# A state-space and feed-forward block on one core: an earlier load, late modulation in steps, and an engine for each PSUM copy

## The chip, the core and the metric

The kernel runs on one core of a Trainium2 chip. The core has a matrix engine (TensorE, PE in the profile; PEld is its weight load), a vector engine (VectorE, DVE), a scalar engine (ScalarE, ACT), GpSimd (POOL) and SyncE (SP), which here only issues transfers. Each engine works through its own instructions in order and waits for others by semaphores. Matmul results land in PSUM, which has banks of 128 x 512 fp32 values; VectorE and ScalarE carry them from there to SBUF. The metric is the device time of one execution in microseconds, as the median of several runs.

## The reference

```python
mod = (silu(c) @ w_mod).reshape(1, 6, 1, -1)
sa, ca, ga, sb, cb, gb = (mod[:, i] for i in range(6))
h = layernorm(x) * (1 + ca) + sa                  # x: 1 x 2048 x 512
x = x + ga * S4(h)
h = layernorm(x) * (1 + cb) + sb
x = x + gb * ((relu(h @ w1 + b1) ** 2) @ w2 + b2) # w1: 512 x 1792

def S4(u):                                        # 512 channels, 128 states each
    dt = exp(log_dt)
    P = exp(dt * A * l)                           # complex A, l = 0 .. 2047
    K = real(sum over n of C * P * (dt * B))      # one kernel of 2048 per channel
    return causal_convolution(u, K) + u * Dskip
```

All values are fp32.

## The kernel before

**Head.** `log_dt` (`ldt`), the vector c (`cin`), the S4 parameters (`prm`, one part of 64 channels and one of 448) and sixteen rows of x are loaded. VectorE forms dt = exp(log_dt) in 14 small operations (L455 to L465); a matmul group (L468) and a ScalarE copy (L471) spread it. `parameters()` (L476 to L542) then makes, from A, B, C and dt, a decay rate, a phase and an amplitude per state, in fp32 products on GpSimd, reciprocals and comparisons on VectorE, and Abs, Sign, Arctan and Sin on ScalarE; it is run for the first 64 channels and for the other 448. Beside it VectorE takes the layernorm statistics of the sixteen rows (L556, L557), and TensorE forms the first three modulation vectors from `w_mod` (L579), which become a gain and a shift per channel (L611 to L616). Sixteen row steps follow (`row_pieces`, L626 to L634): VectorE applies mean, gain and shift, TensorE transposes, ScalarE copies the bank into `xj`. Every block of 64 channels needs all sixteen rows.

**Convolution.** It is done by matmuls against fixed tables of cosines, in 8 blocks of 64 channels. For each block `u_pieces` (capitals A to H) transforms the input in four `stage1` steps (8 matmuls with `d1`, L668, and a bank copy, L670) and four `stage2` steps (16 matmuls with `t2`, L678, and a copy, L701); `swap_piece` (digits) writes by two transfers a copy with halves exchanged (L708); `product_pieces` (small letters a to h) runs `stage2` on the kernel's spectrum, multiplies it with the input's (L814, straight from PSUM), and transforms back with `e1` (L823), whose bank is copied into `z4` in two halves (L829).

The kernel K itself is generated in 32 units of 16 channels. For each unit GpSimd adds phases (L760) and forms amplitudes (L780, L784); ScalarE takes sine and cosine (L770 to L772) into two-bank tiles `tg`; VectorE multiplies (L794 to L797); TensorE contracts over the states into `kg` (L804); the result is copied to `ksb` (L870), the skip weight is added (L871), and `stage1` transforms it (L668, L670). Three further exponent tables (`kgen_exp`, L751) are made on ScalarE on the way. "Late modulation" (`late_modulation`, letter l) makes the second set of modulation vectors.

**Feed-forward.** The inverse transform (L1016) gives the residual x2; it is normalised, transposed and modulated (L1041 to L1053), and the two matrix products run in a seven-product scheme with each fp32 operand split in two reduced-precision parts (L1090 to L1094 and L1132 to L1134, with the splits in `split`, L924 and L925).

**Order.** Three banks named "ps" serve nearly all steps of the convolution. `ORDER` gives for each of the 32 units a string of letters, the pieces to be written out after it. All instructions so written are then put in order by `keep_order` (L159), a list scheduler with its own costs for every instruction: whenever an engine is free, it takes of the ready groups the one that is farthest from the end, and `hurry` adds an offset from `HURRY` (in ns) to that distance for a stretch of the program. SP keeps program order. The resulting order of each engine is fixed when the kernel is built.

## Time and profile before

| what | us |
|---|---|
| median of 3 runs | 624.87 |
| lowest and highest | 624.28, 624.88 |
| span of the profiled execution | 625.9 |
| first row product (L626) starts | 42.2 |
| first stage-one matmul (L668) starts | 67.1 |
| first inverse matmul (L1016) starts | 293.2 |

The profile is of one execution; its span is taken from the first to the last instruction, and it is 1.0 us above the median of the timed runs. The page lists busy time by engine; a view by stages gives busy time of each engine between two times, a view by groups gathers instructions of one line, operation and tile with their mean length and what ended the idle time before them, and the timeline has single instructions. Names in it are those of the kernel without their numbers (`xy<-ps` writes a spectrum from a "ps" bank). Short instructions of one kind overlap a little in their start and end, so the mean length of one is longer than the step from one to the next.

### The profile page before, as it was taken

What the parts mean: (1) busy time and instruction counts of PE and PEld (TensorE: products, weight loads), DVE (VectorE), ACT (ScalarE), POOL (GpSimd) and SP (SyncE); (2) the same over time, 40 slices, a digit from 0 to 9 for tenths busy, and PEclk for the clock granted to TensorE, in tenths of its full rate; (3) what the DMA queues carried; (4) which work ended last, traced back from release to release, by engine and by line L of the source; (5) the groups of instructions that cost most, each with busy time, mean ns of one, the idle gap of its engine ahead of it and who ended that gap; (6) DMA issues with size and microseconds to landing.
All of it is one profiled execution on the core that took longest, in us unless ns stands there. A gap on an engine that the chain in (4) does not pass through costs nothing.

```text
span 625.9 us, 21088 instructions
## 1 busy us (share of the span) xinstructions
PE 566.7 (91%) x9230; PEld 490.4 (78%) x9230; DVE 485.4 (78%) x846; ACT 425.1 (68%) x752; POOL 251.7 (40%) x215
## 2 busy tenths in 40 slices
PE   1338999999999999989699899999999999999996
PEld 1236889899899998988578678888888878888885
DVE  3999968798699979835898998646999886655744
ACT  2966879989989677641575866757666766666530
POOL 3849699899998898471004100000000500000000
PEclk9999999999999999999689999999999999999999
DMA  9940231130303303156206421112521532111432
GB/s 319 398 146 3 70 70 31 45 71 3 72 5 71 67 7 71 31 125 225 85 4 214 147 78 34 35 34 85 186 84 45 174 102 72 47 34 35 144 96 79
DMA packets 31355, 57.00 MB, mean 91 GB/s; under 512 B 4512, under 2 KB 13600, under 8 KB 29856
## 3 DMA queue, kind: packets, MB, share of 16 engines
q1 hardware_dynamic: 30832, 55.53, 29.2%
q8 instruction: 72, 1.18, 0.8%
q10 hardware_dynamic: 432, 0.14, 0.1%
q14 instruction: 19, 0.16, 0.1%
HBM read 43.07 MB, written 4.19 MB: 76 GB/s over the span
## 4 chain that ended last, share of the span: by engine, by line
PE 60%; DVE 18%; ACT 12%; DMA 4%; issue 4%; POOL 0%; SPq 0%; DVEq 0%; ACTq 0%
PE ps L668 7%; PE ps L678 7%; PE ps L823 7%; PE kg L804 4%; PE ps L1090 4%; PE ps L1092 3%; PE ps L1094 3%; PE tg L1132 3%; PE tg L1134 3%; PE tg L1133 3%; DMA work<-w 2%; PE ps L1132 2%; PE ps L1134 2%; PE ps L1133 2%; DVE xy L627 2%
## 5 line engine op out<-in xcount | busy, mean ns | idle before, releaser
L951 POOL TENSOR_TENSOR work<-work 128x256 f32<-128x256 f32 x4 | 3.4, 860 | 195.7 <-DMA work<-w 195.6
L925 DVE TENSOR_TENSOR w2t<-rw,w2t 128x512 fp32r<-128x512 f32 x53 | 37.7, 714 | 39.5 <-ACT w2t L924 39.3
L678 PE MATMUL ps<-xy,t_sb 128*64 128x64 f32 x2048 | 66.8, 223 | 1.7 <-issue 0.7
L678 PEld LDWEIGHTS ps<-xy,t_sb 128*64 128x64 f32 x2048 | 63.9, 138 | 3.6 <-issue 1.0
L924 ACT CAST w2t<-rw 128x512 fp32r<-128x512 f32 x53 | 32.8, 619 | 43.9 <-PE kg L1134 24.3
L823 PE MATMUL ps<-e_sb,xy 128*64 128x128 f32 x1024 | 60.8, 273 | 1.2 <-ACT ksb L870 0.7
L1077 ACT ACTIVATE more<-more,b1c 128x512 f32<-128x512 f32 x54 | 38.9, 720 | 28.8 <-DVE more L1115 16.5
L823 PEld LDWEIGHTS ps<-e_sb,xy 128*64 128x64 f32 x1024 | 56.5, 139 | 2.2 <-ACT ksb L870 0.8
L1132 PE MATMUL tg<-w2t,t2t 128*128 128x512 f32 x112 | 44.0, 392 | 0.8 <-DVE t2t L1084 0.7
L670 ACT COPY xy<-ps 128x512 f32<-128x512 f32 x64 | 36.5, 591 | 11.4 <-PE ps L668 11.3
L1133 PE MATMUL tg<-w2t,t2t 128*128 128x512 f32 x112 | 43.6, 389 | 0.0
L1134 PE MATMUL tg<-w2t,t2t 128*128 128x512 f32 x112 | 43.6, 389 | 0.0
L814 DVE TENSOR_TENSOR xy<-ps,xy 128x512 f32<-128x512 f32 x64 | 40.0, 683 | 0.6 <-issue 0.2
L924 ACT CAST wset<-work 128x512 fp32r<-128x512 f32 (+2 forms) x36 | 24.7, 690 | 22.3 <-DMA work<-w 13.7
L760 POOL TENSOR_TENSOR llph<-lo,big 128x1024 int32<-128x1024 int32 x16 | 34.3, 2146 | 10.6 <-ACT tg L772 10.5
L829 DVE COPY big<-ps 128x256 f32<-128x256 f32 x64 | 24.0, 418 | 16.1 <-PE ps L823 16.1
L1090 PE MATMUL ps<-opt,wset 128*128 128x512 f32 x84 | 34.0, 404 | 2.7 <-ACT more L1101 2.7
L668 PE MATMUL ps<-d_sb,ksb 128*64 128x128 f32 x512 | 34.3, 276 | 1.5 <-DVE ksb L871 1.1
L760 POOL TENSOR_TENSOR rtlph<-lo,big 128x1024 int32<-128x1024 int32 x16 | 34.3, 2145 | 3.2 <-ACT tg L772 2.6
L668 PE MATMUL ps<-d_sb,big 128*64 128x128 f32 x512 | 33.1, 274 | 0.7 <-ACT big L634 0.7
L1132 PE MATMUL ps<-w2t,t2t 128*128 128x512 f32 x84 | 33.5, 399 | 0.0
L1092 PE MATMUL ps<-opt,wset 128*128 128x512 f32 x84 | 32.8, 391 | 0.0
(272 smaller groups left out, 1655.7 us busy)
## 6 DMA issues: line engine op xcount, KB each, us to landing
rw<-w SPq DMA_DIRECT2D x53, 256.0 KB, 2.6
xy<-xy SPq DMA_DIRECT2D x16, 512.0 KB, 6.6
xy<-xt SPq DMA_DIRECT2D x24, 256.0 KB, 5.2
xy<-w_mod SPq DMA_DIRECT2D x6, 1024.0 KB, 8.7
work<-w SPq DMA_DIRECT2D x12, 512.0 KB, 4.3
out_dram<-more SPq DMA_DIRECT2D x14, 256.0 KB, 2.0
t_sb<-c_t SPq DMA_DIRECT2D x1, 2048.0 KB, 16.3
i2c<-c_i SPq DMA_DIRECT2D x2, 1024.0 KB, 5.1
```

Of the source, the lines that this page charges most:

```text
L668: nc.tensor.matmul(ps[64 * r : 64 * r + 64, 128 * i : 128 * i + 128], src[:, i], d1_sb[:, r], start=True, stop=True)
L678: nc.tensor.matmul(ps[64 * r : 64 * r + 64, 64 * i : 64 * i + 64].rearrange("p (h q t) -> p q h t", h=2, t=2), t2_sb[:, 8 * g + i, r], src ...
L760: nc.gpsimd.tensor_tensor(ph.rearrange("p d r (a b) -> p (d r) a b", a=4), bc(low_phase[:, us].rearrange("p d r b -> p (d r) b"), 2, 4), b ...
L814: nc.vector.tensor_mul(product_piece(y, g), ps, piece(x, g))
L823: nc.tensor.matmul(ps[64 * m : 64 * m + 64, 128 * i : 128 * i + 128], pairs(y)[:, g, i // 2, 64 * m : 64 * m + 64, i % 2], e1_sb[:, h], st ...
L924: nc.scalar.copy(hi_, raw_)
L1077: nc.scalar.activation(c, c if src is None else src, AF.Relu, bias=b1c[:, t : t + 1])
L1090: pe.append(nc.tensor.matmul(ps, dst[:, 0, wi, kt], o[:, 0, kt], start=start and kt == 0, stop=False, skip_group_check=on))
L1092: pe.append(nc.tensor.matmul(ps, dst[:, 1, wi, kt], o[:, 0, kt], start=False, stop=False, skip_group_check=on))
L1132: nc.tensor.matmul(to[m], l[:, xs], hi_, start=(t == 0), stop=False),
L1133: nc.tensor.matmul(to[m], h[:, xs], lo_, start=False, stop=False),
L1134: nc.tensor.matmul(to[m], h[:, xs], hi_, start=False, stop=(t == NF - 1))])
```

## The change

`log_dt` is loaded first on ScalarE's queue; c is loaded on SP's queue, ahead of the parameters. The first three `w_mod` loads are written right behind the rows of x, ahead of the skip weights. Ten operations of `parameters()` that GpSimd had, and two of VectorE's, take their engine from a string of letters (v for VectorE, g for GpSimd), and so does one product of the exponent tables, for which all letters are g. Each bank copy of `u_pieces` ("u" and "w"), of the generated kernel ("b"), of its `stage1` ("k") and into `z4` ("z") takes its engine from a string too (a for ScalarE, v for VectorE). Late modulation loads, multiplies and copies one vector per step, in three steps, into whichever spectrum buffer is free. The parameters of the 448 channels are written behind the first modulation. `ORDER` and `HURRY` have new values, and offsets are given for each step of a piece and for each unit.

```diff
-    nc.scalar.dma_start(cin, cvec)
+    nc.sync.dma_start(cin, cvec)
...
+FLAGS = {
+    "z": "vvvvvvvvvvvvavvvvvvvvvvvvvaavvvvaavvvaaavvvvvvaavvvvavavvvvvaava",
+    "u": "aavaaavaavvaaaaaaaaaaaaaavvavava",
+    "w": "aaaavaaaaavaaaaaaaaaaaaavaaavvaa",
+    "k": "aavaaaaaaaaaaaaaaavavaaaaavaaaav",
+    "b": "aavaavaaaaavavvaaaavvavvavvaaava",
+    "p": "vggggvgggvvgggv",
+    "P": "ggggggvggvvgggv",
+    "l": "gggggggg",
+}
...
+        choice = iter(FLAGS["P" if n > 1 else "p"])
+        e = lambda: v if next(choice) == "v" else g
-        g.tensor_mul(al, x[1], dt)
-        g.tensor_mul(x[2], x[2], dt)
+        e().tensor_mul(al, x[1], dt)
+        e().tensor_mul(x[2], x[2], dt)
...
-    def late_modulation():
-        for wm, v in ((wm_sb, sbc), (wm_cb, cbc)):
-            m = bank("ps", PS)
-            mod_rows(wm, m)
...
-        m = bank("ps", PS)
-        mod_rows(wm_next(), m)
-        nc.vector.tensor_copy(gb4, m[:, 0:128])
-        spectra.extend(wms[3:])
+    def late_pieces():
+        for v in (sbc, cbc, gb4):
+            wm = wm_next()
+            m = bank("ps", PS)
+            mod_rows(wm, m)
+            spectra.append(wms[-1])
+            if v is gb4:
+                nc.vector.tensor_copy(gb4, m[:, 0:128])
+            else:
...
+            yield
...
+    def evacuate(kind, i):
+        return nc.scalar.copy if FLAGS[kind][i] == "a" else nc.vector.tensor_copy
...
-        nc.scalar.copy(dst[:, o // 4], ps.rearrange("p (t m) -> p m t", t=4))
+        copy(dst[:, o // 4], ps.rearrange("p (t m) -> p m t", t=4))
...
-            nc.scalar.copy(piece(xs, g), stage2(xs, g))
+            evacuate("w", 4 * c + g)(piece(xs, g), stage2(xs, g))
...
-                copy(z4[r][c][:, :, 4 * g : 4 * g + 4], ps.rearrange("p (d r j) -> p j d r", d=4, r=2)[..., r])
+                evacuate("z", 8 * c + 2 * g + r)(z4[r][c][:, :, 4 * g : 4 * g + 4], ps.rearrange("p (d r j) -> p j d r", d=4, r=2)[..., r])
...
-        nc.scalar.copy(ksb, kps)
+        evacuate("b", u)(ksb, kps)
         nc.vector.tensor_add(ksb[:, :, 63], kps[:, :, 63], ds4[:, 4 * u : 4 * u + 4])
-        stage1(ksb, xks[c], 4 * (u % 4))
+        stage1(ksb, xks[c], 4 * (u % 4), evacuate("k", u))
...
-            hurry(mark, HURRY[24 + (u - 1) // 4])
+            hurry(mark, HURRY[208 + u - 1])
...
-HURRY = (-4656, -29973, 39, -105915, 14765, -285, 3125, -2, -603, 233, 1864, 6642, -284, 13749, 1407, -107, 6332, 4392, -789, 6471, 2150, -1844, 36197, -951, 4, -3620, 2447, 26, 48, 3313, 2804, -1815, 3480, 1763, -1323, -2998, -42956, -65922, 5414, 2, -55525, 18242, 558, -2589, 11726, -30808, -19182, -100632, 13494, 42, 384, 26191, -2479, 22, 47180, -2976)
+HURRY = (
+    -2734, -29053, 1835, -33189, 1141, 1317, 4389, 1058, 25783, 87408, -290, 2028, 67789, -1985, 285, 217,
...
```

The lines below the change move by 30 to 40: L668 and L670 of before are L703 and L705 now, L678 and L701 are L713 and L736, L804 is L839, L814 is L849, L823 and L829 are L858 and L863, L870 is L900, L924 and L925 are L964 and L965, L1016 is L1056.

**ScalarE's queue at the start of the program** (`cin` is c, `ldt` is log_dt, `d_sb` the table of `stage1`, `tables` the exponent tables). Before:

```order
L426 DMA cin<-cvec 128x4
L425 DMA ldt<-log_dt 128x4
L441 DMA d_sb<-c_d 128x256
L570 ACT_TABLE_LOAD
L570 ACTIVATE sl<-cin 128x4
L471 COPY big_83<-ps_150 128x8x64
```

Now:

```order
L454 DMA ldt<-log_dt 128x4
L483 DMA d_sb<-c_d 128x256
L607 ACT_TABLE_LOAD
L607 ACTIVATE sl<-cin 128x4
L513 COPY big_83<-ps_153 128x8x64
```

The load of c has left this queue, and log_dt is its first transfer; the order of before, with c first, was the scheduler's.

**VectorE, fourth unit of the generated kernel** (`rtl` a unit's amplitudes, `tg` sine and cosine, `ksb` the unit's kernel, `mt`, `sbc`, `cbc`, `gb` of late modulation). Before:

```order
L794 SCALAR_TENSOR_TENSOR rtl<-rtl,tg_417 128x16x32
L795 TENSOR_TENSOR rtl<-rtl,tg_417 128x16x64
L531 TENSOR_SCALAR big_83<-big_83 128x7x128
L796 TENSOR_TENSOR rtl<-rtl,tg_418 128x16x32
L797 TENSOR_TENSOR rtl<-rtl,tg_418 128x16x64
L871 TENSOR_TENSOR ksb_824<-kg_351,ds_70 128x4
L652 COPY mt_1029<-ps_151 128x128
```

Now:

```order
L705 COPY xy_95<-ps_154 128x512
L829 SCALAR_TENSOR_TENSOR rtl<-rtl,tg_719 128x16x32
L830 TENSOR_TENSOR rtl<-rtl,tg_719 128x16x64
L900 COPY ksb_822<-kg_303 128x256
L901 TENSOR_TENSOR ksb_822<-kg_303,ds_70 128x4
L831 TENSOR_TENSOR rtl<-rtl,tg_720 128x16x32
L686 COPY mt_1028<-ps_154 128x128
L832 TENSOR_TENSOR rtl<-rtl,tg_720 128x16x64
L705 COPY xy_91<-ps_153 128x512
```

Copies of "ps" banks and of `kg` now stand between the four products of a unit.

**ScalarE at the end of the convolution** (`wset` the first sets of w1). Before:

```order
L670 COPY xy_95<-ps_152 128x512
L924 CAST wset_4554<-work 128x1024
L870 COPY ksb_825<-kg_351 128x256
L670 COPY xy_95<-ps_151 128x512
L921 ACT_TABLE_LOAD
```

Now:

```order
L705 COPY xy_94<-ps_153 128x512
L964 CAST wset_4554<-work 128x1024
L900 COPY ksb_823<-kg_303 128x256
L961 ACT_TABLE_LOAD
L961 ACTIVATE ksb_823<-epsb 128x1
L863 COPY big_83<-ps_153 128x64x4
```

The last kernel unit's copy still follows the wide cast of the first w1 set; the copy of its transform (L670 before) has left for VectorE, and copies into `z4` have come.

More of the change, by code (lines that the diff above doesn't have):

```diff
@@ L431, in load_parameters, with wm_load, wm_next @@
         nc.sync.dma_start(raw[:, c0 : c0 + n, 0:6], prm[:, c0 : c0 + n])
+    heads = [spectrum() for _ in range(4)]
+    rows = [runs(t)[:, 512 * i : 512 * i + 512] for t in heads for i in range(4)]
     load_parameters(0, 1)
     load_parameters(1, NC - 1)
-    heads = [spectrum() for _ in range(4)]
-    rows = [runs(t)[:, 512 * i : 512 * i + 512] for t in heads for i in range(4)]
-    for k, t in enumerate(heads):
-        for i in range(4):
-            nc.sync.dma_start(rows[4 * k + i], xt[4 * k + i])
+    for s, row in enumerate(rows):
+        nc.sync.dma_start(row, xt[s])
+    wmod_v = w_mod.rearrange("(k p) c -> p k c", p=P)
+    def wm_load(dst, i):
+        nc.sync.dma_start(dst, wmod_v[:, :, 512 * i : 512 * i + 512])
+    wms = []
+    def wm_next():
+        wms.append(spectrum())
+        wm = wms[-1].rearrange("p a b c -> p (a b c)").rearrange("p (a b) -> p a b", a=4)
+        wm_load(wm, len(wms) - 1)
+        return wm
+    wm_sa, wm_ca, wm_ga = (wm_next() for _ in range(3))
     nc.scalar.dma_start(d1_sb, c_d1.rearrange("p (r m) -> p r m", r=2))
@@ L560, in tile_adaln_ssm_ffn @@
     hurry(mark, HURRY[1])
-    for c, n in ((1, 7),):
-        mark = len(nc.cur_bb.bb.instructions)
-        for _ in parameters(c, n):
-            pass
-        hurry(mark, HURRY[2])
     sl = ctile("sl", [P, 4])
@@ L581, in mod_rows @@
                     start=(kc == 0), stop=(kc == 3))
-    wmod_v = w_mod.rearrange("(k p) c -> p k c", p=P)
-    def wm_load(dst, i):
-        nc.sync.dma_start(dst, wmod_v[:, :, 512 * i : 512 * i + 512])
     srep = ctile("srep", [P, 128])
     nc.vector.tensor_copy(srep.rearrange("p (k x) -> p k x", k=4), bc(sl, 2, 32))
-    wms = []
-    def wm_next():
-        wms.append(spectrum())
-        wm = wms[-1].rearrange("p a b c -> p (a b c)").rearrange("p (a b) -> p a b", a=4)
-        wm_load(wm, len(wms) - 1)
-        return wm
-    wm_sa, wm_ca, wm_ga = (wm_next() for _ in range(3))
     nc.sync.dma_start(t2_sb, c_t2.rearrange("p (k r m) -> p k r m", k=32, r=2))
@@ L620, in tile_adaln_ssm_ffn @@
     spectra.extend(wms[0:3])
-    wm_sb, wm_cb = (wm_next() for _ in range(2))
+    for c, n in ((1, 7),):
+        mark = len(nc.cur_bb.bb.instructions)
+        for _ in parameters(c, n):
+            pass
+        hurry(mark, HURRY[2])
     def row_pieces():
@@ L852, in exp_pieces @@
             yield
-    work = {"l": late_pieces(), "r": row_pieces(), "x": exp_pieces()}
+    work = {"l": late_pieces(), "R": row_pieces(), "x": exp_pieces()}
     work.update((chr(65 + c), u_pieces(c)) for c in range(NC))
@@ L869, in finish, with hurry_piece @@
         ksb = ring(kp, "ksb", 2, [P, 4, 64])
-        nc.scalar.copy(ksb, kps)
+        evacuate("b", u)(ksb, kps)
         nc.vector.tensor_add(ksb[:, :, 63], kps[:, :, 63], ds4[:, 4 * u : 4 * u + 4])
-        stage1(ksb, xks[c], 4 * (u % 4))
+        stage1(ksb, xks[c], 4 * (u % 4), evacuate("k", u))
+    done = {}
+    def hurry_piece(mark, t):
+        done[t] = done.get(t, 0) + 1
+        if t in PIECES:
+            hurry(mark, HURRY[64 + 8 * PIECES.index(t) + done[t] - 1])
+    for t in HEAD:
+        mark = len(nc.cur_bb.bb.instructions)
+        next(work[t])
+        hurry_piece(mark, t)
     next(work["x"])
@@ L888, in tile_adaln_ssm_ffn @@
             kq[u] = rl
-            hurry(mark, HURRY[32 + u // 4])
+            hurry(mark, HURRY[240 + u])
         mark = len(nc.cur_bb.bb.instructions)
```

58 lines of the change are left out of this document (28 added, 30 removed), and 16 rows, old and new, of the table HURRY.

## Prediction

> **What bounds the kernel now.** I read the page first, then busy time by stage, then the head of the timeline, then the idle columns of the TensorE groups. The page alone misleads a little:
>
> ```profile
> span 625.9 us, 21088 instructions
> PE 566.7 (91%) x9230; PEld 490.4 (78%) x9230; DVE 485.4 (78%) x846; ACT 425.1 (68%) x752; POOL 251.7 (40%) x215
> PE 60%; DVE 18%; ACT 12%; DMA 4%; issue 4%; POOL 0%; SPq 0%; DVEq 0%; ACTq 0%
> ```
>
> TensorE is the main bound, but 18% of the chain is VectorE. I cut the span at the first row product, the first stage-one matmul, the first inverse matmul and the feed-forward part (columns: window, length, then busy us and instructions of PE, PEld, DVE, ACT, POOL; then clock, DMA share, GB/s):
>
> ```profile
> 12.20:42.20 30.00, 8.16 (x107) 6.63 (x108) 28.33 (x71) 26.03 (x100) 19.35 (x28) 1.00 0.91 327
> 42.20:67.10 24.90, 20.26 (x519) 16.54 (x518) 24.34 (x36) 12.18 (x20) 22.91 (x20) 1.00 0.01 3
> 67.10:293.20 226.10, 219.53 (x6250) 208.18 (x6250) 180.19 (x295) 176.88 (x286) 188.98 (x138) 1.00 0.26 64
> 293.20:325.00 31.80, 24.33 (x819) 19.52 (x820) 25.48 (x61) 18.94 (x34) 0.00 (x0) 0.79 0.19 60
> 325.00:360.00 35.00, 33.17 (x383) 26.25 (x382) 31.66 (x45) 25.02 (x42) 9.57 (x7) 1.00 0.51 163
> 360.00:625.90 265.90, 259.22 (x1149) 211.54 (x1147) 192.75 (x320) 164.02 (x271) 8.18 (x7) 0.99 0.26 80
> ```
>
> From 12.2 to 67.1 us VectorE is the bound (52.67 of 54.9 us busy), and TensorE cannot start the convolution before the sixteenth row is done. From 67.1 on TensorE is busy 219.53 of 226.10 us, so at most 6.6 us of plain idleness can be won there. A second bound comes from the pace of undisturbed runs in the chain of waits:
>
> ```profile
> 70.02 1.05 PE kg L804 x64
> 232.69 4.82 PE ps L678 x160
> 285.56 7.17 PE ps L823 x128
> ```
>
> That is 16.4, 30.1 and 56.0 ns each. With 2048 of L804, 2048 of L678, and 1024 each of L823 and L668 (taken at L823's pace) it is 33.6 + 61.6 + 114.7 = 209.9 us, and with about 3 us for late modulation 213. So 13 us is all that any order can win in this stage.
>
> **Part 1: log_dt first.** The opening of the timeline (start, length, engine, line, operation; in brackets the idle time before):
>
> ```profile
> 0.73 0.41 ACTq L426 DMA_DIRECT2D cin<-cvec  x1
> 1.17 0.45 ACTq L425 DMA_DIRECT2D ldt<-log_dt  x1
> 3.89 0.20 ACT L570 ACTIVATE sl<-cin 128x4 f32<-128x4 f32 x1 [0.35 <-DMA cin<-cvec]
> 6.59 0.17 DVE L455 TENSOR_SCALAR kf<-ldt 128x4 f32<-128x4 f32 x1 [5.61 <-DMA ldt<-log_dt]
> 12.22 1.69 DVE L486 SCALAR_TENSOR_TENSOR big<-big 128x448 f32<-128x448 f32 x2 [2.85 <-ACT big L471]
> 28.44 1.96 DVE L500 SCALAR_TENSOR_TENSOR big<-big 128x64 f32<-128x64 f32 x2
> 28.84 1.07 POOL L780 TENSOR_TENSOR rtlph<-tables 128x512 f32<-128x512 f32 x1
> 30.32 0.61 DVE L501 SCALAR_TENSOR_TENSOR big<-big 128x448 f32<-128x448 f32 x1
> 30.96 0.63 DVE L509 TENSOR_TENSOR big<-big 128x448 f32<-128x448 f32 x1
> 32.90 0.16 DVE L509 TENSOR_TENSOR big<-big 128x64 f32<-128x64 f32 x1
> 42.20 1.39 DVE L626 SCALAR_TENSOR_TENSOR xy<-xy,mv,kg 128x512 f32<-128x512 f32 x2
> ```
>
> The two loads are of one size, and the first of the ACT queue's pair had landed by 3.89, the second by 6.59. With log_dt first (issued at 0.73, and c moved to SP's queue) I let it land where c did: 2.7 us earlier. The chain behind it (14 small VectorE operations, a matmul group, one copy) ends in L486 5.6 us later and moves whole, to about 9.5. Two other loads are passed on the way. The parameters now queue behind c on SP, some 0.4 us later; their row below gives 7.3 us to landing, so from an issue near 1.6 they are there at 8.9, still ahead of 9.5. The rows of x follow at the same places as before, and VectorE never waited for one.
>
> ```profile
> big<-prm SPq DMA_DIRECT2D x1, 1344.0 KB, 7.3
> xy<-w_mod SPq DMA_DIRECT2D x6, 1024.0 KB, 8.7
> ```
>
> From 12.2 on VectorE has no slack to lose, so the 2.7 us reach the first row product, corrected by what changes on VectorE: three parameter products come from POOL, two 64 wide at 0.16 and one 448 wide at 0.63, +0.95. Two L500 took 1.96 us where their neighbours L501 and L509 take 0.6 for the wide form: some 1.1 us were lost while POOL's L780 ran. In the new order POOL ends its products and those three L780 while VectorE is still in the row statistics, so this stall may go; I take half, -0.55. Head: -2.7 + 0.95 - 0.55 = **-2.3 us**. Bounds: -2.9 with the whole stall gone, and +0.5 if log_dt gains only its 0.44 us of issue time.
>
> The Trainium skill, in "DMA: Bandwidth & Descriptors", section "Issuing engines are not separate DMA queues", says that transfers issued by different engines run on the same 16 DMA engines and interleave, and that issuing from several saves only the issue time. By it the move of c to SP's queue is worth 0.4 us and no more, and the head would come out at +0.5; it speaks against the 2.7, unless log_dt's being ahead of the parameters' bytes is what counts. The two landings above, 3.1 and 5.4 us after their issues, bear that reading out.
>
> **Part 2: products off POOL.** POOL loses 1.8 us in a stretch where it is busy 19.35 of 30; hidden by VectorE's queue. Without that cover it would be a gain.
>
> **Part 3: PSUM copies by engine.** The groups of the convolution (busy, mean | idle before, by releaser):
>
> ```profile
> L678 PE MATMUL ps<-xy,t_sb 128*64 128x64 f32 x2048 | 66.8, 223 | 1.7 <-issue 0.7 <-DVE big L829 0.5 <-ACT xy L670 0.4
> L823 PE MATMUL ps<-e_sb,xy 128*64 128x128 f32 x1024 | 60.8, 273 | 1.2 <-ACT ksb L870 0.7 <-ACT xy L670 0.5
> L668 PE MATMUL ps<-d_sb,ksb 128*64 128x128 f32 x512 | 34.3, 276 | 1.5 <-DVE ksb L871 1.1 <-ACT xy L670 0.2
> L668 PE MATMUL ps<-d_sb,big 128*64 128x128 f32 x512 | 33.1, 274 | 0.7 <-ACT big L634 0.7
> L814 DVE TENSOR_TENSOR xy<-ps,xy 128x512 f32<-128x512 f32 x64 | 40.0, 683 | 0.6 <-issue 0.2 <-PE ps L678 0.2
> L670 ACT COPY xy<-ps 128x512 f32<-128x512 f32 x64 | 36.5, 591 | 11.4 <-PE ps L668 11.3
> L829 DVE COPY big<-ps 128x256 f32<-128x256 f32 x63 | 23.7, 418 | 16.1 <-PE ps L823 16.1
> L870 ACT COPY ksb<-kg 128x256 f32<-128x256 f32 x32 | 12.0, 374 | 12.4 <-PE kg L804 12.4
> L795 DVE TENSOR_TENSOR rtl<-rtl,tg 128x1024 f32<-128x1024 f32 x11 | 13.4, 1215 | 0.4 <-POOL rtl L784 0.4
> ```
>
> The letters move 18 copies of 512 columns (8 "u", 5 "w", 5 "k") and 12 of 256 ("b") from ScalarE to VectorE, and 15 of 256 ("z") the other way. ScalarE: -18 x 0.591 - 12 x 0.374 + 15 x 0.374 = -9.5 us, from 176.9 to 167. VectorE has no 512-wide copy here; the nearest row that reads a bank of that width is L814: 18 x 0.683 + 12 x 0.418 - 15 x 0.418 = +11.0, from 180.2 to 191 of 226. Both stay below TensorE's 213, so the sums decide nothing; only waits do. Of TensorE's idle time ScalarE ended 2.5 us; 0.7 of it is the start of the stage and stays, 1.8 can go. The rest of the 13 us is slow pace and not idleness; I take the share of the stage in which ScalarE was full (over 9.9) and VectorE had room (under 8.6), six of 23 stretches of ten us, such as these:
>
> ```profile
> 110.00:120.00 10.00, 9.60 (x234) 9.13 (x234) 6.87 (x15) 9.94 (x29) 8.25 (x8) 1.00 0.22 56
> 120.00:130.00 10.00, 9.69 (x303) 8.96 (x293) 8.54 (x14) 9.97 (x16) 10.00 (x7) 1.00 0.02 5
> ```
>
> 6/23 of the 6.5 is 1.7. Convolution: -1.8 - 1.7 = **-3.5 us**, bounds -13 and, by the rival below, +9.
>
> What stays late is the tail. The copy of the last kernel block waits behind a ScalarE cast for the first w1 set, and the new order has the two rows in the same sequence:
>
> ```profile
> 274.52 1.05 ACT L924 CAST wset<-work 128x1024 fp32r<-128x1024 f32 x1 [1.60 <-POOL work L954]
> 275.47 0.37 ACT L870 COPY ksb<-kg 128x256 f32<-128x256 f32 x1
> 276.09 1.09 PE L668 MATMUL ps<-d_sb,ksb 128*64 128x128 f32 x16 [1.15 <-DVE ksb L871]
> ```
>
> So I take nothing for it.
>
> **Part 4: late modulation in three steps.** Two rows of the chain of waits bear on it:
>
> ```profile
> 65.40 1.11 PE ps L631 x32
> 83.25 1.05 PE kg L804 x64
> ```
>
> Its three loads now go into the row buffers, the last of which is free only when the sixteenth row's matmuls are through, at 66.5 - 2.3 = 64.2; 8.7 us to landing gives 73. Its matmuls stand behind the third L804 (83.25 now, about 81 then) and later. On SP's queue only the first swap stands behind the loads, and it follows a whole spectrum. The cover is 8 us; taken at 0, and each us that it falls short by would stand on TensorE.
>
> **Part 5: feed-forward.** TensorE's order from the first inverse matmul to the end is the same, row for row. VectorE adds the rows of x earlier. TensorE has 6.7 us of idleness after 360, mostly waits of fractions; 0, with 1.5 us either way.
>
> **Sum.** The profiled execution: 625.9 - 2.3 - 3.5 = 620.1. The median of the runs shown lies 1.0 us below that span, so **619.1 us**.
>
> **Rivals.** *Head only:* the new order of the convolution wins and loses alike, 624.87 - 2.3 = 622.6; for it, TensorE is already at 97% there. *All idleness goes:* -2.3 - 6.6, 616.0, and at row pace down to 609.5; for it, ScalarE's relief falls on the stretches where it was full; against it, 2 us of the idleness is ended by VectorE, which gets more to do. *log_dt lands no earlier*: the parameters' 1344 KB hold it up wherever it is issued, so -0.44 + 0.95 in the head and nothing in the convolution, 625.4; against it, c landed in 3.1 us beside the same parameters. (This is the case of the Trainium skill's rule above, "DMA: Bandwidth & Descriptors".) *VectorE holds the banks:* there are three "ps" banks, and a moved copy waits in VectorE's queue behind products of up to 1.215 us, half of that on average; 30 copies x 0.61 = 18.2 us. If TensorE has another bank ready only half the time, 9.1 surface: 624.87 - 2.3 + 9.1 = 631.7, slower. It decides from 0.12 us per copy ((2.3 + 1.25) / 30). Against it: 32 matmuls into a bank last 0.96 (L678) to 1.79 us (L823), so two other banks cover a mean wait.
>
> **How the numbers follow.** Forecast 0.42 (own range 617 to 621.5), head only 0.18, all idleness 0.18, no earlier landing 0.10, held banks 0.12. 0.2% is 1.25 us, about what a measurement here can tell from nothing. Faster: 0.42 + 0.18 + 0.18 = 0.78; same 0.10; slower 0.12. Range 613 to 625: it takes in all but the held banks and the far end of the third case.
>
> **What would show it.** log_dt ends VectorE's first wait near 4; L530 starts near 9.5; the first row product near 39.9; the first L703 near 64.8; the first inverse matmul near 287.4, with ScalarE about 167 and VectorE about 191 us busy in between; 332.7 us from there to the end. Wrong if L530 stays near 12, if TensorE's idle time names L705, L736 or L900 on VectorE as its releaser for more than 3 us, or if the stretch from the first inverse matmul changes by over 1.5 us.

## The result, and the profile after

The changed kernel takes 623.0 us (median of 20 runs, 619.0 to 625.6) beside 626.35 us for the kernel before (20 runs, 621.7 to 627.7): a ratio of 0.9947, 95% interval 0.9932 to 0.9963. It is faster, by 3.3 us where 5.8 were forecast, and the time lies 3.9 us above the 619.1 forecast.

The page of the changed kernel:

```profile
span 620.6 us, 21074 instructions
PE 562.8 (91%) x9230; PEld 487.7 (79%) x9230; DVE 497.8 (80%) x864; ACT 416.7 (67%) x737; POOL 249.1 (40%) x212
PE 60%; DVE 21%; ACT 8%; issue 4%; DMA 4%; POOL 2%; DVEq 0%; SPq 0%; POOLq 0%; ACTq 0%
```

ScalarE's share of the chain went from 12% to 8%, VectorE's from 18% to 21%. The span is 5.3 us shorter than that of the profile before, yet the medians differ by 3.3. Where an execution is on record with both a time and a span, the time is 1.7 to 2.1 us more than the span, mostly 1.8 (622.40 and 620.6 here). The time of the execution that was profiled before is not on record; by this difference its span of 625.9 answers to about 627.7 us, as long as the longest of the 20 (627.65) and 1.3 above their median. The prediction had set its span against the median of three runs.

The stages of the changed kernel, cut as before at the parameters' first product, the first row product, the first stage-one matmul and the first inverse matmul (window, length, busy us and instructions of PE, PEld, DVE, ACT, POOL, then clock, DMA share, GB/s):

```profile
8.59:39.52 30.93, 6.79 (x106) 5.79 (x107) 28.25 (x75) 25.76 (x100) 17.57 (x25) 0.89 0.83 301
39.52:64.59 25.07, 20.28 (x520) 16.59 (x518) 24.41 (x36) 12.07 (x20) 22.77 (x20) 0.86 0.27 87
64.59:287.75 223.16, 217.74 (x6251) 206.86 (x6252) 191.69 (x310) 169.16 (x270) 188.40 (x138) 1.00 0.26 65
287.75:620.60 332.85, 315.92 (x2348) 256.66 (x2348) 249.82 (x423) 207.67 (x346) 17.61 (x14) 0.98 0.28 87
```

And its head in the timeline:

```profile
0.73 0.41 ACTq L454 DMA_DIRECT2D ldt<-log_dt  x1
0.74 0.39 SPq L455 DMA_DIRECT2D cin<-cvec  x1
2.59 0.78 DVE L497 TENSOR_SCALAR kf<-ldt 128x4 f32<-128x4 f32 x1 [1.61 <-DMA ldt<-log_dt]
8.59 0.23 DVE L530 SCALAR_TENSOR_TENSOR big<-big 128x64 f32<-128x64 f32 x1 [2.10 <-ACT big L513]
39.52 0.73 DVE L655 SCALAR_TENSOR_TENSOR xy<-xy,mv,kg 128x512 f32<-128x512 f32 x1
```

log_dt is there 4.0 us earlier (2.59 against 6.59), the first product 3.6 (8.59 against 12.22), the first row product 2.7 (39.52 against 42.20). Then the convolution is 2.9 us shorter (223.16 against 226.06), and behind it nothing changes (332.85 against 332.67). So this pair of profiles bears out the sum of the prediction, stage by stage, and the medians do not. That gap is what most runs below are about.

### The profile page after: what moved, and what is told of

The parts are those of the page before. It is cut to its first block, busy times and chain, and to the rows that moved or that the text cites. A ratio compares the mean times of both kernels' runs of the same rounds, so it can differ in the third digit from the quotient of the medians.

```text
span 620.6 us, 21074 instructions
## 1 busy us (share of the span) xinstructions
PE 562.8 (91%) x9230; PEld 487.7 (79%) x9230; DVE 497.8 (80%) x864; ACT 416.7 (67%) x737; POOL 249.1 (40%) x212
## 4 chain that ended last, share of the span: by engine, by line
PE 60%; DVE 21%; ACT 8%; issue 4%; DMA 4%; POOL 2%; DVEq 0%; SPq 0%; POOLq 0%; ACTq 0%
PE ps L703 7%; PE ps L858 7%; PE ps L713 7%; PE kg L839 4%; PE ps L1130 3%; PE ps L1132 3%; PE ps L1134 3%; PE tg L1172 3%; PE tg L1173 3%; PE tg L1174 3%; PE ps L1172 2%; PE ps L1174 2%; PE ps L1173 2%; PE tg L1056 2%; DVE xy L656 2%
## 5 line engine op out<-in xcount | busy, mean ns | idle before, releaser
L965 DVE TENSOR_TENSOR w2t<-rw,w2t 128x512 fp32r<-128x512 f32 x53 | 37.8, 716 | 38.9 <-ACT w2t L964 38.6
L713 PE MATMUL ps<-xy,t_sb 128*64 128x64 f32 x2048 | 65.8, 223 | 1.2 <-ACT xy L705 0.7
L713 PEld LDWEIGHTS ps<-xy,t_sb 128*64 128x64 f32 x2048 | 63.2, 138 | 3.2 <-ACT xy L705 0.9
L964 ACT CAST w2t<-rw 128x512 fp32r<-128x512 f32 x53 | 32.8, 619 | 45.1 <-PE kg L1174 24.5
L858 PE MATMUL ps<-e_sb,xy 128*64 128x128 f32 x1024 | 61.1, 274 | 0.9 <-DVE xy L849 0.9
L1117 ACT ACTIVATE more<-more,b1c 128x512 f32<-128x512 f32 x54 | 38.9, 721 | 28.9 <-DVE more L1155 16.6
L858 PEld LDWEIGHTS ps<-e_sb,xy 128*64 128x64 f32 x1024 | 56.1, 139 | 2.1 <-DVE xy L849 1.0
L1172 PE MATMUL tg<-w2t,t2t 128*128 128x512 f32 x112 | 43.9, 392 | 0.3 <-DVE t2t L1124 0.2
L849 DVE TENSOR_TENSOR xy<-ps,xy 128x512 f32<-128x512 f32 x64 | 39.7, 681 | 1.7 <-ACT xy L736 1.1
L705 ACT COPY xy<-ps 128x512 f32<-128x512 f32 x51 | 29.2, 588 | 15.0 <-PE ps L703 14.8
L964 ACT CAST wset<-work 128x512 fp32r<-128x512 f32 (+2 forms) x36 | 24.5, 689 | 16.5 <-DMA work<-w 7.3
L703 PE MATMUL ps<-d_sb,ksb 128*64 128x128 f32 x512 | 33.5, 275 | 0.9 <-DVE ksb L901 0.9
L703 PE MATMUL ps<-d_sb,big 128*64 128x128 f32 x512 | 32.6, 274 | 1.8 <-DVE big L863 1.1
L1172 PE MATMUL ps<-w2t,t2t 128*128 128x512 f32 x84 | 33.4, 398 | 0.0
L1174 PE MATMUL ps<-w2t,t2t 128*128 128x512 f32 x84 | 32.8, 391 | 0.0
```

The costliest lines, as they stand in the source:

```text
L703: nc.tensor.matmul(ps[64 * r : 64 * r + 64, 128 * i : 128 * i + 128], src[:, i], d1_sb[:, r], start=True, stop=True)
L713: nc.tensor.matmul(ps[64 * r : 64 * r + 64, 64 * i : 64 * i + 64].rearrange("p (h q t) -> p q h t", h=2, t=2), t2_sb[:, 8 * g + i, r], src ...
L849: nc.vector.tensor_mul(product_piece(y, g), ps, piece(x, g))
L858: nc.tensor.matmul(ps[64 * m : 64 * m + 64, 128 * i : 128 * i + 128], pairs(y)[:, g, i // 2, 64 * m : 64 * m + 64, i % 2], e1_sb[:, h], st ...
L964: nc.scalar.copy(hi_, raw_)
L1117: nc.scalar.activation(c, c if src is None else src, AF.Relu, bias=b1c[:, t : t + 1])
```

## The experiments

All runs in one place. A block is what was run together on one chip, with its own runs of the kernel before; the stages are of the one profiled execution of each run.

| run (block) | median, runs | ratio to before, 95% | first row product | convolution | from the first inverse matmul to the end |
|---|---|---|---|---|---|
| before | 626.35, 20 | 1 | 42.20 | 226.06 | 332.67 |
| changed kernel | 623.00, 20 | 0.9947 (0.9932 to 0.9963) | 39.52 | 223.16 | 332.85 |
| b_again (1) | 625.23, 12 | 1.0001 (0.9981 to 1.0020) | 41.18 | 226.40 | 332.05 |
| a_again (1) | 621.16, 10 | 0.9938 (0.9915 to 0.9960) | 39.53 | 223.03 | 333.52 |
| h_undo (1) | 623.96, 12 | 0.9975 (0.9954 to 0.9996) | 42.34 | 222.23 | 330.83 |
| p_undo (1) | 621.83, 7 | 0.9939 (0.9915 to 0.9964) | 39.09 | 222.83 | 332.96 |
| f_undo_p (2) | 656.62, 5 | 1.0464 (1.0440 to 1.0487) | 39.40 | 245.08 | 334.52 |
| g_only_p (2) | 644.54, 5 | 1.0272 (1.0253 to 1.0291) | 42.55 | 240.05 | 335.62 |
| ffn_before (2) | 622.11, 7 | 0.9936 (0.9909 to 0.9962) | 39.51 | 223.30 | 331.02 |
| h_only_p (2) | 628.12, 12 | 1.0014 (0.9996 to 1.0032) | 39.43 | 226.12 | 337.14 |
| h_exact (3) | 622.59, 6 | 0.9932 (0.9908 to 0.9955) | 38.79 | 226.81 | 331.82 |
| f_undo_x (3) | 632.36, 6 | 1.0107 (1.0085 to 1.0129) | 39.52 | 233.64 | 332.02 |
| g_only_x (3) | 626.17, 12 | 0.9998 (0.9981 to 1.0015) | 41.70 | 225.53 | 332.78 |
| ffn_after_in_before (3) | 626.01, 12 | 0.9999 (0.9981 to 1.0016) | 41.86 | 227.55 | 332.01 |
| a_3 (4) | 622.03, 12 | 0.9949 (0.9928 to 0.9971) | 39.49 | 223.01 | 333.41 |
| h_exact_2 (4) | 621.33, 12 | 0.9948 (0.9925 to 0.9971) | 38.77 | 226.39 | 329.45 |
| ffn_before_2 (4) | 620.96, 6 | 0.9924 (0.9896 to 0.9951) | 39.51 | 223.12 | 331.50 |
| best (4) | 620.10, 8 | 0.9915 (0.9887 to 0.9944) | 39.07 | 223.46 | 330.87 |
| best_2 (5) | 620.02, 6 | 0.9893 (0.9869 to 0.9917) | 39.07 | 224.32 | 330.31 |
| a_4 (5) | 621.85, 6 | 0.9923 (0.9898 to 0.9949) | 39.51 | 224.71 | 331.11 |

### Both kernels again

No edit.

> The kernel before, unchanged, timed against itself: ratio 1.000 within 0.002 in any theory. It gives a second profile. Theory A (the first profile of before fell on a long execution, 625.9 us of span where the median of its runs answers to about 624.6, and the convolution is what varies from execution to execution): span near 624.6, first row product near 42.2, first stage-one matmul near 67.1, 332.7 us from the first inverse matmul to the end, and the convolution 1 to 1.5 us shorter than 226.06. Theory B (it is the head that varies, with the landing of log_dt): L486 starts 1 us or more away from 12.22, the convolution is again 226.

> The changed kernel, unchanged: 0.9947 of before in any theory (0.993 to 0.997). A second profile. Theory A: L530 near 8.6, first row product near 39.5, first L703 near 64.6, 332.8 us from the first inverse matmul to the end, and the convolution 0.5 to 1 us longer than 223.16. Theory B: the first row product 1 us or more later than 39.52, the convolution near 223.2.

Of the kernel before, in the timeline of its second profile:

```profile
5.57 0.17 DVE L455 TENSOR_SCALAR kf<-ldt 128x4 f32<-128x4 f32 x1 [4.59 <-DMA ldt<-log_dt]
11.20 1.69 DVE L486 SCALAR_TENSOR_TENSOR big<-big 128x448 f32<-128x448 f32 x2 [2.85 <-ACT big L471]
```

log_dt landed a full microsecond earlier than in the first profile, and all of the head moved with it: theory B is right of the head of before, which is one of the things that vary. (Four profiles have that head unaltered: first row product at 42.20, 41.18, 41.70 and 41.86, mean 41.74.) In the changed kernel, where log_dt is first, it does not vary: 39.49 to 39.53 in the seven profiles with that head, although the first operation on log_dt starts anywhere from 2.54 to 2.90 in them; why is told under part 1 below. Theory A is wrong of the convolution in these two profiles: it did not shrink in the second one of before, nor grow in that of the changed kernel. The profiles of later blocks show that it does vary somewhat, from 226.1 to 227.6 us with the orders and engines of before and from 222.2 to 224.7 with those of the changed kernel.

### The head undone, and done alone

h_undo, on the changed kernel:

```diff
+    nc.scalar.dma_start(cin, cvec)
     nc.scalar.dma_start(ldt, log_dt)
-    nc.sync.dma_start(cin, cvec)
```

> The changed kernel with the two small loads as before, c first and log_dt second, both on ScalarE's queue; TensorE's order is unchanged. Theory A: log_dt lands near 6.6, L530 starts near 12.2, and the loss reaches the end: 2.6 us slower than the changed kernel, 0.9988 of before. Theory B (the head of the changed kernel is worth little): 0 to 1 us slower than the changed kernel, 0.995 to 0.996 of before. Rival: the transfers' place decides nothing but the 0.44 us of issue time: 0.995 to 0.996 too, with L530 near 9.1, which the profile tells from theory B.

The first row product was back at 42.34, 2.8 us later, and the median 2.8 us above that of a_again in the same block (2.3 by the means). Theory A's head term stands.

h_only_p and h_exact, on the kernel before:

```diff
-    nc.scalar.dma_start(cin, cvec)
+    nc.sync.dma_start(cin, cvec)
```

> The kernel before with c moved to SyncE's queue, so that log_dt is first on ScalarE's; TensorE's order is held at that of before, VectorE's and ScalarE's in the head are made anew. Theory A: log_dt has landed by 2.6, L486 starts near 8.6, and without the three products that the changed kernel moves to VectorE the first row product starts near 38.7 (41.2 and 42.2 in the two profiles of before); the whole gain reaches the end, ratio 0.995 to 0.996. Rival (a landing 3 us earlier is lost in the wait for the parameters or in the statistics): first row product at 40.5 or later, ratio 0.998 or more.

The head did as theory A says but for 0.7 us, and the run as a whole gained nothing: the rival's ratio, but not for the rival's reason. The scheduler was free there to set every engine's rows but TensorE's, and it set those of the feed-forward part worse. Windows from its first stage-one matmul on, then two rows of TensorE's waits behind the first inverse matmul (us in total, times, longest):

```profile
64.14:290.26 226.12, 219.85 (x6251) 207.95 (x6251) 181.11 (x295) 176.94 (x285) 188.74 (x138) 1.00 0.26 64
290.26:627.40 337.14, 317.84 (x2348) 256.68 (x2348) 250.30 (x424) 207.51 (x345) 17.64 (x14) 0.98 0.28 86
```

```profile
PE ps L1090 <- ACT more L1101: 4.1, 4, 1.5
PE tg L1046 <- ACT xy L1041: 0.9, 1, 0.9
```

337.14 us with TensorE's own rows unchanged: the sequence on the other engines alone is worth about 4.8 us there, and in the time, set against h_exact below (1.0014 and 0.9932), about as much. So from here on the sequences were held: a list gives the order of all groups of instructions in the kernel that an experiment starts from, and each engine takes its own in that order.

> The kernel before with one edit: c is loaded on SyncE's queue ahead of the parameters. Every engine's rows stand in the sequence of before (in the earlier try with this edit the scheduler was free to set the other engines' rows, and the feed-forward part became 4.8 us longer, 337.14 against 332.05 to 332.67). Theory A: L486 near 8.6, first row product near 38.8, convolution 226.2, 332.4 us from the first inverse matmul to the end: 0.995 to 0.9955 of before. Rival F (an earlier start of the feed-forward part is given back there, since something in it does not move with the head): head as said, feed-forward part 1.5 us or more longer, ratio 0.997 or more.

> The kernel before with the early load of log_dt alone, every engine's rows in the sequence of before, a second time. Theory T: 0.9955 of before (2.9 us, the whole of it in the head). Rival G: 0.993 again (4.2 us), as fast as the changed kernel. Its convolution takes 226.1 to 227.5 us in either.

The timeline of h_exact, and its windows:

```profile
2.60 0.77 DVE L455 TENSOR_SCALAR kf<-ldt 128x4 f32<-128x4 f32 x1 [1.61 <-DMA ldt<-log_dt]
8.83 1.69 DVE L486 SCALAR_TENSOR_TENSOR big<-big 128x448 f32<-128x448 f32 x2 [2.85 <-ACT big L471]
38.79 1.39 DVE L626 SCALAR_TENSOR_TENSOR xy<-xy,mv,kg 128x512 f32<-128x512 f32 x2
```

```profile
8.83:38.79 29.96, 8.16 (x107) 6.63 (x108) 28.30 (x72) 26.03 (x100) 19.31 (x28) 1.00 1.00 363
290.58:622.40 331.82, 316.30 (x2348) 256.69 (x2348) 250.03 (x424) 207.60 (x345) 17.93 (x14) 0.98 0.28 87
```

One moved load, and nothing else, gives 0.9932 and 0.9948: the same as the whole change within what these runs can tell. Its 18 runs have a mean of 622.1 us (standard error 0.4), the 48 runs of the changed kernel 622.2 (0.2); beside each other in block 4 they have 622.0 and 622.1. The head alone moved by 3.0 us (38.79 against the mean of 41.74), a ratio of 0.9953, which lies within both intervals. So theory T, by which the changed kernel is 2 us or more faster than the early load alone, does not hold.

### The parameter products back on GpSimd

p_undo, on the changed kernel:

```diff
-    "p": "vggggvgggvvgggv",
-    "P": "ggggggvggvvgggv",
+    "p": "gggggggggvvgggg",
+    "P": "gggggggggvvgggg",
```

> The changed kernel with all parameter products back on GpSimd, as before; TensorE's order is unchanged. By the prediction's term VectorE gets 0.95 us less to do in a head that it bounds: 0.9 us faster than the changed kernel, 0.9932 of before, first row product near 38.6. Rival: GpSimd becomes what VectorE waits for there (VectorE already waits 1.04 us for the product L536 at 15.3 and 0.78 for L574 at 37.4): no gain, or up to 1.5 us slower than the changed kernel, with longer waits on POOL tiles ahead of VectorE's L552 and L575.

The strings decide fourteen operations (twelve of them GpSimd's before, not ten, and two VectorE's); three of these change sides here. The first row product came 0.43 us earlier (39.09), about half of the 0.9 that the prediction's term gives; ahead of it VectorE now waits 1.55 us for TensorE's L639, the matmuls that spread gain and shift; the rival had foreseen a new wait, but on GpSimd.

```profile
39.09 2.06 DVE L655 SCALAR_TENSOR_TENSOR xy<-xy,mv,kg 128x512 f32<-128x512 f32 x3 [1.55 <-PE kg L639]
```

In the time 0.4 us cannot be told from nothing.

### Engines for the bank copies, without the new order and the other way round

f_undo_p and f_undo_x, on the changed kernel; g_only_p and g_only_x have the opposite edit on the kernel before (the changed kernel's five strings, and the copies made through them):

```diff
-    "z": "vvvvvvvvvvvvavvvvvvvvvvvvvaavvvvaavvvaaavvvvvvaavvvvavavvvvvaava",
-    "u": "aavaaavaavvaaaaaaaaaaaaaavvavava",
...
+    "z": "vvvvvvvvvvvvvvvvvvvvvvvvvvvvvvvvvvvvvvvvvvvvvvvvvvvvvvvvvvvvvvvv",
+    "u": "aaaaaaaaaaaaaaaaaaaaaaaaaaaaaaaa",
...
```

In the two with _p TensorE's rows are held and the scheduler sets the others; in the two with _x all rows keep their place in time, and only the copies change sides.

> The changed kernel with every bank copy of the convolution on the engine it had before (u, w, k, b on ScalarE, z on VectorE); TensorE's order is held at that of the changed kernel, the other engines' orders are made anew by the scheduler. Theory C (the choice of engine brings the 3 us, as the prediction says): the stretch from the first stage-one matmul to the first inverse matmul is again 226 us (223.0 to 223.2 in the changed kernel), ScalarE about 176 us busy in it, and the run is 3 us slower than the changed kernel, 0.999 of before. Rival O (the new order of the pieces brings it): the stretch stays near 223.2 and the ratio near 0.994. Rival H (held banks): the stretch is shorter than 223, 221 or less, since the copies leave VectorE's queue.

> The kernel before with the changed kernel's engines for the bank copies and nothing else; TensorE's order is held at that of before. Theory C: the stretch from the first stage-one matmul to the first inverse matmul falls from 226.1 to 223, with ScalarE about 167 and VectorE about 191 us busy in it, 0.995 of before. Rival O: it stays near 226 and the ratio at 1.000. Rival H: it grows, to 228 or more, with TensorE idle ahead of matmuls that VectorE's copies release, ratio above 1.003.

f_undo_p is some 33 us slower than the changed kernel, g_only_p 17 us slower than the kernel before: no theory had that. Part of it is the scheduler's, which sets ScalarE's and VectorE's rows by distance from the end and does not know that TensorE's are held (with all rows held the two edits cost 10 us and nothing, see below), so these two runs decide nothing. The stricter pair does.

> The changed kernel with the bank copies of the convolution on the engines of before, each at its old place in time: every engine's rows stand in the sequence of the changed kernel, and only the 45 copies change sides. Theory C (the choice of engine brings the 3 us): the stretch from the first stage-one matmul to the first inverse matmul is near 226.3 (223.0 to 223.2 in the changed kernel). Rival O (the order of the pieces brings them): 223.0 to 223.7. Rival S (order and engines fit only together, as the 32 and 17 us of the two earlier tries suggest): 230 or more, with TensorE idle ahead of matmuls that ScalarE's copies L705 and L736 release.

> The kernel before with the changed kernel's engines for the bank copies, each copy at its old place in time; every engine's rows stand in the sequence of before. Theory C: 223 us from the first stage-one matmul to the first inverse matmul (226.1 and 226.4 in before). Rival O: 225.7 to 226.7. Rival S: 230 or more.

The convolution of f_undo_x and of g_only_x:

```profile
64.84:298.48 233.64, 220.92 (x6251) 208.96 (x6251) 179.27 (x294) 177.29 (x285) 188.83 (x138) 0.99 0.25 63
```

```profile
66.69:292.22 225.53, 219.11 (x6251) 207.68 (x6252) 188.91 (x310) 170.08 (x270) 188.83 (x138) 1.00 0.25 64
```

In the old order the new engines are worth 0.5 to 0.9 us in the profile and nothing in the time (0.9998), though they move ScalarE and VectorE by 7 to 9 us each: theory C falls. In the new order the old engines cost 10 us. Rival S is right for that half. The largest of the waits in f_undo_x shows why (timeline of ScalarE, VectorE and TensorE):

```profile
106.27 5.69 ACT L786 ACTIVATE tables<-big 128x128 f32<-128x128 f32 x24
111.77 0.40 ACT L900 COPY ksb<-kg 128x256 f32<-128x256 f32 x1
```

```profile
112.20 0.16 DVE L901 TENSOR_TENSOR ksb<-kg,ds 128x4 f32<-128x4 f32 x1 [6.33 <-ACT ksb L900]
114.01 0.75 DVE L863 COPY big<-ps 128x256 f32<-128x256 f32 x2
```

```profile
114.81 5.38 PE L858 MATMUL ps<-e_sb,xy 128*64 128x128 f32 x64 [4.29 <-DVE big L863]
```

A kernel block's copy (L900) that is put on ScalarE stands behind a series of 24 exponent tables. VectorE, which adds the skip weight to it, waits 6.33 us with its own queue behind it; in that queue is the copy that frees TensorE's bank; TensorE waits 4.29 us. So the strings of engines are no gain by themselves: the new order, in the sequence that it has, depends on them. Whether another sequence of ScalarE's and VectorE's rows would let it run as fast with the engines of before was not tried, beyond the scheduler's own in f_undo_p.

What the new order brings can be read from the two profiles. Some of TensorE's waits in the convolution, of before and then of the changed kernel (us in total, times, longest):

```profile
PE ps L668 <- DVE ksb L871: 1.1, 1, 1.1
PE ps L823 <- ACT ksb L870: 0.7, 1, 0.7
PE ps L823 <- ACT xy L670: 0.5, 1, 0.5
PE ps L678 <- ACT xy L670: 0.4, 2, 0.2
```

```profile
PE ps L703 <- DVE big L863: 1.1, 1, 1.1
PE ps L703 <- DVE ksb L901: 0.9, 1, 0.9
PE ps L858 <- DVE xy L849: 0.9, 1, 0.9
PE ps L713 <- ACT xy L705: 0.7, 1, 0.7
```

Taken over the stage alone, all listed waits together are 6.0 and 5.3 us. Those that ScalarE ended fell from 1.8 to 0.7 and those put down to "issue" from 1.7 to 0.9, but those that VectorE ended rose from 2.5 to 3.7. Gaps too short to be listed fell by 0.4, and most of the 2.9 us is busy time (219.54 to 217.74). Counted in TensorE's timeline, the old order goes from one kind of matmul to another 149 times in this stretch and the new one 134 times, and the step from one matmul to the next has a median of 149 ns where the kind changes, against means of 16 to 54 ns within a kind. Fifteen changes at about 0.1 us are an estimated 1.5 us, most of the 1.8. That is worked out, not tried apart, and it cannot be all that sets the busy time: f_undo_x has the changed kernel's order of matmuls and 220.92 us.

### The sequence of rows in the feed-forward part

From the first inverse matmul on TensorE's rows are the same in both kernels, as the prediction says. ScalarE's and VectorE's are not: 53 of 342 and 106 of 420 groups stand elsewhere. ffn_before gives the changed kernel the old sequence, ffn_after_in_before the kernel before the new one; best is ffn_before with the strings of p_undo.

```diff
+        able = {e: [g for g in r if g < TAIL or g == TAIL + chain[e][0]] for e, r in ready.items()}; first = {e: min(r) if e == "SP" else min(r, key=lambda g: at[g]) for e, r in able.items() if r}
...
+TAIL = 1190
+CHAIN = {
+    "PE": (
...
```

> The changed kernel with the rows of every engine from the first inverse matmul on in the sequence of before (TensorE's was the same already; 53 of ScalarE's 342 groups and 106 of VectorE's 420 stand elsewhere in the changed kernel). Theory E (the new sequence on ScalarE and VectorE costs 0.8 us in the feed-forward part: 332.85, 333.52 and 332.96 us from the first inverse matmul to the end against 332.67 and 332.05 before): near 332.3 from there to the end, no wait over 0.3 us ahead of the first row L1130 some 79 and 94 us after the first inverse matmul, and 0.8 us faster than the changed kernel, 0.9925 to 0.993 of before. Rival (the difference is chance from execution to execution): 332.4 to 333.6 and the ratio at 0.994.

> The kernel before with the rows of every engine from the first inverse matmul on in the sequence of the changed kernel (TensorE's is the same). Theory E (that sequence costs about 1 us): 333 us or more from the first inverse matmul to the end, waits of 0.4 us or more ahead of the L1090 rows some 79 and 94 us after the first inverse matmul, ratio 1.001 to 1.003. Rival (chance): 332.0 to 332.7, no such waits, ratio 1.000.

> The changed kernel again, beside the early load alone on the same chip. Theory T (the 3 us that the profiles show in the convolution reach the end): 2 to 2.5 us faster than the early load alone, first matmul of the inverse near 287.7, 333 us behind it. Rival G (they are given back behind the convolution): within 0.8 us of the early load alone, with 1.5 us more than there from the first inverse matmul to the end.

> The changed kernel with the rows behind the first inverse matmul in the sequence of before, a second time and beside the changed kernel. Theory E (the new sequence of ScalarE's and VectorE's rows is where it is given back): 1 us or more faster than the changed kernel, no waits ahead of L1130 some 79 and 94 us after the first inverse matmul, 331 to 332 us from there to the end. Rival: within 0.6 us of it, the stretch at 333.

> The changed kernel with the parameter products back on GpSimd (first row product 0.44 us earlier, 39.09) and the rows behind the first inverse matmul in the sequence of before. Theory E: 1.4 us faster than the changed kernel, 0.9915 of before. Rival: 0.4 us faster, 0.9935.

> The version with the parameter products on GpSimd and the old sequence of rows in the feed-forward part, a second time. Theory E: 1.4 us faster than the changed kernel beside it; 331 us from the first inverse matmul to the end. Rival: 0.4 us faster or less; 332.5 or more.

> The changed kernel beside it: 0.9945 of before within 0.002, 333 us from the first inverse matmul to the end with waits ahead of L1130 some 79 and 94 us after it (theory E), or 331 to 332 and none (rival: chance).

Two rows of TensorE's waits behind the first inverse matmul, of the changed kernel and then of ffn_before:

```profile
PE ps L1130 <- ACT more L1141: 3.8, 4, 1.4
PE tg L1172 <- DVE t2t L1124: 0.2, 1, 0.2
```

```profile
PE ps L1130 <- ACT more L1141: 2.1, 2, 1.1
PE tg L1172 <- DVE t2t L1124: 1.2, 1, 1.2
```

The two waits at 79 and 94 us behind the first inverse matmul are gone (0.9 and 0.5 us in the changed kernel); the one at L1172 grows from 0.2 to 1.2 us instead. Of five profiles with the new sequence (changed kernel, a_again, a_3, a_4, p_undo) the stretch has a mean of 332.8 us, of four with the old one (ffn_before twice, best twice) 330.9. Two more profiles fit less well: f_undo_x has the new sequence and 332.02, and h_undo, where only a few rows stand elsewhere than in it, has 330.83, in the shortest of its twelve runs.

Only part of the 1.9 us is steady. From the 820th to the 1351st matmul of the stretch, some 31 to 101 us behind the first inverse matmul, the six profiles of the changed kernel's orders with the new sequence take 70.4 to 70.9 us (mean 70.7), the four with the old one 69.7 to 70.4 (70.0). In h_undo, whose few other rows also take away the wait at 79 us, it is 69.4. The rest lies in the first 31 us, which vary by 2.3 us between a_3 and a_4, one and the same kernel. a_4, run to decide between the theories, gave half an answer to each: both waits are there (0.9 and 0.5 us), as theory E says, and the stretch is 331.11, as the rival says, since its waits put down to "issue" in the first 31 us are the shortest of all (1.9 us).

In time, ffn_before_2 is 1.1 us below a_3 beside it, best 1.9 below a_3, best_2 1.8 below a_4; all 14 runs of best have a mean of 620.4 (standard error 0.4) against 622.2 (0.2) of the changed kernel. All 82 runs of the changed kernel, p_undo, ffn_before and best together, each set against the kernel before in its own block and with the products' share taken apart, give 1.2 us to the old sequence, with a standard error of 0.4. best is the fastest kernel here: 0.9915 and 0.9893 of before. The windows of best:

```profile
8.59:39.07 30.48, 7.92 (x106) 6.52 (x107) 27.68 (x71) 25.86 (x100) 20.56 (x30) 1.00 0.85 306
287.23:618.10 330.87, 316.03 (x2348) 256.64 (x2348) 250.26 (x423) 208.09 (x346) 17.99 (x14) 0.98 0.28 87
```

So theory E is borne out for the changed kernel, with its early start and its convolution, at about 1 us; the least of it is seen in the ratios of ffn_before alone (0.9936 and 0.9924 against 0.9923 to 0.9949), whose intervals overlap. It does not hold in general: in the kernel before the new sequence costs nothing (0.9999, 332.01 us). And single executions of one kernel differ by up to 2.4 us in this stretch (a_again 333.52, a_4 331.11).

## Why the prediction was right and wrong

**The base was wrong, and it is most of the miss in the time.** The last step of the sum, "The median of the runs shown lies 1.0 us below that span", took a long execution for a usual one. Time is span plus about 1.8 us; the sum of 620.1 us of span means 621.9 us, not 619.1. The measured 623.0 lies 1.1 above that. Three runs (624.28 to 624.88) had looked tighter than the kernel is: 20 range from 621.7 to 627.7. The change of 5.8 us that the terms add up to does not hold this error, and of it only 3.3 came. Of the 2.5 that are missing, the head accounts for 0.1 (2.2 of 2.3, below), the convolution for 0.6 (2.9 of 3.5), and what is left, some 1.8 us by difference, is for the stretch behind them, where the prediction had put 0 (part 5).

**Part 1, -2.3 us: right in size, by errors that cancel.** The landing gained 4.0 us in that pair of profiles, not 2.7: log_dt was in by 2.59, earlier than c had been. The chain behind it did not move whole, as the prediction had it: its first operation, L497, took 0.78 us where it had taken 0.17, and ended at 3.37, just behind a series of GpSimd MEMSETs (3.34). In all fourteen profiles with log_dt first it ends at 3.36 or 3.37, whether it starts at 2.54 or at 2.90, and that is why the head does not vary there; that the MEMSETs hold it up was not tried. The first product moved by 3.6 us for it. The stretch from the first product to the first row product grew by 0.95 (29.98 to 30.93), not by 0.40. The stall of L500 (L544 now) went whole, and not by half. The three products cost 1.9 us by their rows (L531, L537 and L536), not 0.95, and a new wait of 1.04 us on a GpSimd product came with them; VectorE's busy time in the stretch stayed the same (28.33 and 28.25). The head moved by 2.7 us in the pair, 2.2 against the mean of before. The timeline of the changed kernel:

```profile
1.41 1.93 POOL L767 MEMSET tables<- 128x128 f32 x8
3.40 0.17 DVE L498 TENSOR_SCALAR kf<-kf 128x4 f32<-128x4 f32 x1
8.73 0.34 DVE L531 TENSOR_TENSOR big<-big 128x64 f32<-128x64 f32 x1
16.39 0.73 DVE L537 TENSOR_TENSOR big<-big 128x448 f32<-128x448 f32 x1 [1.04 <-POOL big L536]
17.64 0.83 DVE L536 TENSOR_TENSOR big<-big 128x64 f32<-128x64 f32 x1
27.16 0.56 DVE L544 SCALAR_TENSOR_TENSOR big<-big 128x448 f32<-128x448 f32 x1
```

The rival that log_dt lands no earlier is refuted: 1.8 us from issue to landing, where 5.4 stood. The prediction read a price of +0.5 for the head out of the Trainium skill ("DMA: Bandwidth & Descriptors", "Issuing engines are not separate DMA queues"), where issuing from several engines saves only the issue time. The head moved by -2.7, so that price is refuted here; the other reading that the prediction left open, that what is ahead counts, agrees with the rows. log_dt is now issued at 0.73 and the parameters at 1.19, where it had been issued at 1.17 and the parameters at 0.74. No run moved the parameters alone.

**Part 2: hidden, as said.** With the three products back on GpSimd the head is 0.43 us shorter and not longer.

**Part 3, -3.5 us: right in size (2.9 in the pair), wrong in its reasons.** The busy times came out as said (ScalarE 169, VectorE 192 us). But of the 1.8 us of waits on ScalarE that "can go" 1.1 went, and VectorE's took their place. Relief of ScalarE alone does not win the 1.7 us of slow pace: g_only_x has it and wins 0.5 to 0.9 us of profile and no time. Most of what fell would answer to fewer changes of matmul kind, by the estimate above. That the engines bring nothing in the old order, and that the new order loses 10 us without them, was not among the rivals. Held banks, the rival on the slow side, did not come: with 45 copies moved and the order of before, the convolution got no longer (225.53).

**Part 4, 0: right.** In the changed kernel SyncE issues the three loads from 52.57 to 64.3 us; the first of their matmuls starts at 79.89, later ones stand at 84.35 in the chain of waits, and none waits for a load:

```profile
52.57 11.75 SPq L472 DMA_DIRECT2D xy<-w_mod  x3
84.35 1.75 PE ps L616 x63
```

**Part 5, 0: this is the step that failed in the kernel itself.** "TensorE's order from the first inverse matmul to the end is the same, row for row" was true and not enough: ScalarE and VectorE were busy 208 and 250 of 333 us there, their order had changed, and it costs the changed kernel about 1 us (1.2 by the times, 0.7 of it steady in the profiles). The profile pair hid this (332.67 and 332.85), since the one of before is of a long execution: the prediction's own sign, a change of over 1.5 us in this stretch, did not show in that pair. Set against the early load alone, the account is this: head 0.7 us later (39.52 against 38.79), convolution 3.1 shorter (223.5 against 226.6, means of the changed kernel's four profiles and of h_exact's two), feed-forward part 2.1 longer (332.7 against 330.6, the same means), -0.3 in all, where the times say 0.1 with a standard error of 0.4. So what the new order wins in the convolution is given back, about a quarter in the head and the rest behind it. How the second part is made up is shown only roughly: the two profiles of h_exact differ by 2.4 us there, and 1.0 of the 2.1 us lies in the steady stretch from 31 to 101 us.

**Open.** In five profiles of kernels with the old order of matmuls and the old feed-forward sequence (before, b_again, g_only_x and the h_exact pair) the stretch behind the first inverse matmul runs from 329.45 to 332.78. Of the two profiles of before, the first lay 1.3 us above the median of the 20 runs and the second 1.2 above that of its own twelve. The first 31 us of the stretch vary most (28.9 to 32.6 us). TensorE's waits there that the profile puts down to "issue" are 5.3 to 6.7 us in fifteen of 18 profiles (all but f_undo_p and g_only_p), and 4.4, 3.1 and 1.9 in best_2, h_exact_2 and a_4. One more thing goes along with it: over 35 us from the first inverse matmul the granted clock is 0.80 in eight of the 18 profiles and 0.85 in ten, and the first 31 us take 31.7 and 30.2 us on average. Here are a_3 and a_4, one kernel, in that window:

```profile
287.39:322.39 35.00, 27.71 (x953) 21.70 (x953) 28.36 (x63) 20.62 (x37) 0.00 (x0) 0.80 0.18 56
289.29:324.29 35.00, 29.22 (x1007) 22.45 (x1009) 29.80 (x66) 22.10 (x40) 0.00 (x0) 0.85 0.17 55
```

a_4 has issued 54 matmuls more by its end. Whether the clock makes the waits longer or the waits lower the clock was not tried.

## What to carry to other kernels

Before a sum is set against a median, put the profiled execution among the timed ones: its own time, not its span, and more than three of them. An unchanged row order on the bounding engine says little; compare the engines that release it too, since their sequence alone was worth 1 to 5 us here. Take the smallest part of a large change by itself, with all orders held: here one moved load was worth as much as the whole.
